# Attention scores per head in row tiles of the TensorE array, beside a mixture of experts

## The chip, the core and the metric

The kernel runs on one core of a Trainium2 chip. The time is the device time of one execution in microseconds (us). The core has five engines that run side by side: PE (TensorE, the matrix array, whose weight loads are listed as PEld), DVE (VectorE), ACT (ScalarE), POOL (GpSimd) and SP (SyncE, which here issues all DMAs).

## The reference

One layer norm feeds two branches, whose outputs are added to the input:

```python
xn = _layernorm(x, axis=-1)                    # x: 1 x 2048 x 512
# A: 32 heads of 16, causal window of 256
scores = jnp.einsum("bhqd,bhkd->bhqk", q, k) * (Dh ** -0.5)
mask = (idx[:, None] - idx[None, :] >= 0) & (idx[:, None] - idx[None, :] < W)
p = _softmax(jnp.where(mask[None, None], scores, -1e9), axis=-1)
o = jnp.einsum("bhqk,bhkd->bhqd", p, v)        # then @ wo
# B: 8 experts, F = 1376, all 8 with softmax gates
h = _silu(xf @ w1[e]) @ w2[e]
out = out + w * h
return x + _A_ref(xn, A_wqkv, A_wo) + _B_ref(xn, B_w_gate, B_w1, B_w2)
```

## The kernel before

Float32 products are made of float16 halves: each operand is split into a high and a low part, and three matmuls (high x high, high x low, low x high, `mm3`, lines 210 to 212) give one product. For the queries and keys of a head the three products are stacked along the contraction instead: 3 x 16 = 48 rows (`KR`), and two more rows (`QR` = 50) that subtract the row's maximum in the second pass.

The experts take most of the time. A loop over "doubles" (`first_products`) computes the first products with a seven-multiplication scheme (tiles zx and zy, 256 columns per matmul), and queues the second products (tile acc, 512 or 256 columns), which are drained between them. Attention is a third stream of work. It is cut into steps, and after each product `beside` lets it take as many as its share of the remaining work demands (`attend_due`). The order on every engine is worked out when the program is built: `Order` keeps a planned clock for each engine, PE matmuls advance it by a cost written beside them (`order.pe(...)`), and a step is only taken when what it needs is done by that clock. What is issued runs in that fixed order, with semaphores where a tile is handed on. Four PSUM banks (`take_bank`) are shared by the attention tiles and the experts' tanh tiles.

Attention works on one pair of heads and one half of the sequence (1024 queries) at a time: 2 x 16 passes.

- `stacks_of` loads q and k of the pair. Head a lies in rows 64a to 64a + 49. The q tile is block diagonal: its columns alternate between 64 queries of head 0 and 64 queries of head 1, and the rows of the other head are zero (`of_head` picks every second run of 64 columns). So each q load is made of pieces of 64 elements, and two ZERO loads clear the rows of the maxima.
- `att_max` finds each row's maximum. For each of 16 blocks of 64 queries one matmul (line 1947, tile sc) has 64 queries of both heads as its 128 output rows and up to 320 keys as columns; DVE adds the mask and reduces (line 1935). The maxima are transposed (tile mT, line 1954) and put into q (line 1970). This runs for the next pair beside `att_out` of the present one.
- `att_out` makes the scores again, transposed: 128 keys as output rows, and 128 or 256 queries of one head as columns (line 2072, tile st). An item of up to four 128-column pieces fills one bank and holds both heads: 11 items in the first half of the sequence, 13 in the second. ACT takes the exponential into pf (line 2028), POOL masks the newest and oldest blocks (lines 2012 and 2019), ACT makes the high part ph (line 2034), DVE or POOL the low part pl (line 2038). `LAG` items later the pv matmuls follow (line 2109, 34 columns each).
- `att_wo` projects four pairs' outputs.

The steps of `att_max` and `att_out` are interleaved by `attention`, with the constants `LEAD` and `SLACK`.

Of the kernel before, what the change touches and what calls it, by code (L numbers as in the profile page):

```python
# [10 lines left out]
F32 = mybir.dt.float32  # L11
# [32 lines left out]
LAG = 3  # L44
PB = 9
ITEMS = (11, 13)
# [7 lines left out]
LEAD = 5  # L54
SLACK = 4
# [146 lines left out]
def tile_attn_moe(ctx: ExitStack, tc: tile.TileContext, x, wqkv, wo, _bx, wg, w1, w2, out):  # L202
# [18 lines left out]
    ZERO = dram.tile([2, HALF], F16, name="ZERO")  # L221
# [305 lines left out]
    class Stream:  # L527
# [21 lines left out]
        "att": H // 2 * sum(n + QB + 2 * QB + 1 for n in ITEMS) + H // 8 * 2 * 10,  # L549
# [684 lines left out]
    for b in range(2):  # L1234

        qt = att.tile([P, 2 * HALF], F16, name=f"q{b}")
        nc.vector.memset(qt, 0.0)
        qst.append(qt)
        kt = att.tile([P, NK], F16, name=f"k{b}")
        nc.gpsimd.memset(kt, 0.0)  # L1240
        kst.append(kt)
# [14 lines left out]


    def of_head(ap, a):

        return ap.rearrange("r (b c) -> r b c", c=P)[:, :, 64 * a : 64 * a + 64]  # L1260
# [4 lines left out]
    def stacks_of(hf, p, slack):  # L1265

        s = Pair()
        s.hf, s.p = hf, p
        t0 = hf * HALF
        s.k0 = max(0, t0 - WIN)  # L1270
        s.nk = t0 + HALF - s.k0
        s.q, s.k = qst[p % 2], kst[p % 2]
        qf, kf = s.q, s.k
        s.free = [Event(order.t + DRAIN)]
        parts = []

# [12 lines left out]
        return s  # L1289

    with tc.tile_pool(name="ph0", bufs=1) as p0:
# [496 lines left out]
        def gates_out(tb, pool, tag):  # L1788
            yield [gated[tb], bank_free]
            ps, until = take_bank("gp")  # L1790
            for i in range(4):
                nc.tensor.transpose(ps[:E, i * P : (i + 1) * P], gates[:, 4 * tb + i, :], ident)

            def out():
                gs = pool().tile([P, TB], F32, tag=tag, bufs=3 if tag == "pf" else 2, name="gs")
# [39 lines left out]
        fill = p0.tile([P, 2, 20], F16, name="fill")  # L1835
        for j, (t, val) in enumerate(((ZERO, 0.0), (ONE, CO))):
            n = t.shape[0] * t.shape[1] // P
            nc.vector.memset(fill[:, j, :n], val)
            nc.sync.dma_start(t.rearrange("r t -> (r t)").rearrange("(p c) -> p c", p=P), fill[:, j, :n])
# [89 lines left out]
    def att_max(s):  # L1929
# [4 lines left out]
        def best(ps, n, j):  # L1934
            nc.vector.tensor_tensor_reduce(  # L1935
                out=ps[:, :n], in0=ps[:, :n], in1=maskf[:, MB * 64 - n :], scale=1.0, scalar=-3.0e38,
                op0=ALU.add, op1=ALU.max, accum_out=mt[:, j : j + 1],
            )

        for j in range(2 * QB):  # L1940
            jb = 2 * s.hf * QB + j
            kb = max(0, jb + 1 - MB)
            n = (jb - kb + 1) * 64
            cs = kb * 64 - s.k0
            yield [s.loaded, bank_free]
            ps, until = take_bank("sc")
            nc.tensor.matmul(  # L1947
                ps[:, :n], lhsT=s.q[:, j * P : (j + 1) * P], rhs=s.k[:, cs : cs + n], start=True, stop=True
            )
            found.append(order.task("V", 95 + n, partial(best, ps, n, j), [order.pe(n * 3 // 7)], 2500))  # L1950
            until(found[-1])
# [14 lines left out]
        def put():  # L1966
            for a in range(2):
                for r, src in enumerate((mh, ml)):
                    row = 64 * a + KR + r
                    nc.sync.dma_start(of_head(s.q[row : row + 1, :], a), src[:, 64 * a : 64 * a + 64])  # L1970
# [10 lines left out]
    def items_of(hf):  # L1981

        first, last = hf * QB, hf * QB + QB - 1
        near = {kb: [(kb, a, d) for a in range(2) for d in range(2) if first <= kb + d <= last]
                for kb in range(max(first - 1, 0), last + 1)}
        items = []
        for kb in range(max(first - 2, 0), last - 1, 2):
            items += [near.pop(n) for n in list(near) if n <= kb + 2 - (first > kb)]
            items.append([(kb + m, a, 2) for m in range(2) for a in range(2)])
        return items + list(near.values())  # L1990

    def att_out(s, quad):
# [6 lines left out]
        for n, item in enumerate(items):  # L1999
            for c, (kb, a, d) in enumerate(item):  # L2000
                place[kb, a, d] = (n, c)
                used[n] = max(used.get(n, 0), kb + d - first)
        made = []

        def selects(item, w):

            ds = [d for _, _, d in item]
            m = len(item)

            def newest():  # L2010
                pf = w["pf"][:, : m * P].rearrange("p (a c) -> p a c", a=2)[:, :, :P]
# [12 lines left out]
            return [(390, newest)] * (0 in ds) + [(610, oldest)] * (2 in ds)  # L2024

        def exp(ps, n, w):
            w["pf"] = at.tile([P, 4 * P], F32, tag="pf", bufs=3, name="pf")
# [32 lines left out]
        for n_item, item in enumerate(items):  # L2060
            n = len(item) * P
            yield [s.ready, bank_free]
            ps, until = take_bank("st")
            c = 0
            while c < len(item):
                kb, a, d = item[c]
                m = 1
                while c + m < len(item) and item[c + m][:2] == (kb, a):
# [8 lines left out]
            w = {"gone": Event()}  # L2077
            made.append(w)
            m = len(weighed)
            old = [weighed[m - 3]["low"]] if m >= 3 else []  # L2080
            t = last_exp = order.task(
                "A", 160 + n * 5 // 6, partial(exp, ps, n, w), [order.pe(n * 7 // 16), last_exp, *old], 2500
            )
            until(t)
            for cost, what in selects(item, w):
                t = order.task("G", cost, what, [t], 4000)
            old = [weighed[m - PB]["gone"]] if m >= PB else []
            if m:
                old.append(weighed[m - 1]["high"])
            w["high"] = order.task("A", 100 + n * 5 // 6, partial(high, n, w), [t, *old], 5500)  # L2090
            w["low"] = order.either({"V": 80 + n, "G": 80 + n * 41 // 20}, partial(low, n, w), [w["high"]], 7500)
            weighed.append(w)

            def whole(q):
                return max(place[k][0] for k in place if k[0] + k[2] == first + q)

            while done < QB and (n_item == len(items) - 1 or n_item >= LAG + max(whole(q) for q in range(done // GJ * GJ, done // GJ * GJ + GJ))):
                ns = sorted({place[k][0] for k in place if k[0] + k[2] == first + done})
                yield [s.v_at, *(made[i]["low"] for i in ns), *([bank_free] if done % GJ == 0 else [])]
# [5 lines left out]
                for a in range(2):  # L2105
                    ops = [(b, part) for b in kbs for part in ("hi", "lo")]
                    for n, (b, part) in enumerate(ops):
                        i, c = place[b, a, jb - b]
                        nc.tensor.matmul(  # L2109
                            pv[:, 2 * (done % GJ) + a, :], lhsT=made[i][part][:, c * P : (c + 1) * P],  # L2110
# [3 lines left out]
                for i in ns:  # L2114
                    if used[i] == done:
                        made[i]["gone"].end = ev.end
# [60 lines left out]
    def attention():  # L2177
# [8 lines left out]
        for n, (hf, p) in enumerate(todo):  # L2186
# [10 lines left out]
            speed = (2 * QB + 1 + (10 if p % 4 == 0 and n else 0)) / (steps - LEAD - SLACK)  # L2197
# [59 lines left out]
```

## Time and profile before

| | |
|---|---|
| median of 3 runs | 2098.97 us (2095.89 to 2101.11) |
| span of the profiled execution (its only time on record) | 2094.1 us |
| TensorE busy | 99% (17924 matmuls) |
| DVE, ACT, POOL busy | 80%, 67%, 53% |
| DMA | 279.29 MB, 45.7% of the 16 engines |
| granted TensorE clock | 1.00 throughout |

The span runs from the first to the last instruction. An engine's busy time is the union of its instructions; on TensorE the instructions overlap each other, and their ends are modelled. In a group's row, "x448 | 130.6, 299 | 2.0 <-DVE mt" means 448 instructions, 130.6 us busy, 299 ns for one on average, and 2.0 us in which the engine stood idle before them, most of it released by DVE's write of mt. The forms "128*128 128x320" are stationary tile (contraction rows * output rows) and output.

### The profile page before, as it was taken

What the parts mean: (1) busy time and instruction counts of PE and PEld (TensorE: products, weight loads), DVE (VectorE), ACT (ScalarE), POOL (GpSimd) and SP (SyncE); (2) the same over time, 40 slices, a digit from 0 to 9 for tenths busy, and PEclk for the clock granted to TensorE, in tenths of its full rate; (3) what the DMA queues carried; (4) which work ended last, traced back from release to release, by engine and by line L of the source; (5) the groups of instructions that cost most, each with busy time, mean ns of one, the idle gap of its engine ahead of it and who ended that gap; (6) DMA issues with size and microseconds to landing.
All of it is one profiled execution on the core that took longest, in us unless ns stands there. A gap on an engine that the chain in (4) does not pass through costs nothing.

```text
span 2094.1 us, 47341 instructions
## 1 busy us (share of the span) xinstructions
PE 2065.3 (99%) x17924; PEld 1519.3 (73%) x17924; DVE 1665.6 (80%) x3689; ACT 1408.4 (67%) x2566; POOL 1114.5 (53%) x1228
## 2 busy tenths in 40 slices
PE   7999999999999999999999999999999999999999
PEld 4656666787768876886666688667876787668865
DVE  8667777798779867987778899869978798779853
ACT  5747776567756776667758667766687667766752
POOL 5534665456635655545535655554565466555631
PEclk9999999999999999999999999999999999999999
DMA  6886444344434445344456544443444334444321
GB/s 221 259 247 202 115 142 126 80 149 132 142 83 146 117 110 150 117 118 136 114 129 188 140 135 131 131 125 99 137 147 126 101 112 134 127 117 133 87 80 51
DMA packets 287827, 279.29 MB, mean 133 GB/s; under 512 B 128328, under 2 KB 189768, under 8 KB 287600
## 3 DMA queue, kind: packets, MB, share of 16 engines
q1 hardware_dynamic: 287600, 276.28, 45.7%
q8 instruction: 140, 2.29, 0.5%
q14 instruction: 87, 0.71, 0.1%
HBM read 250.42 MB, written 25.50 MB: 132 GB/s over the span
## 4 chain that ended last, share of the span: by engine, by line
PE 79%; DVE 5%; DMA 2%; ACT 1%; SPq 1%; issue 1%; POOL 1%; DVEq 0%; POOLq 0%; ACTq 0%
PE acc L210 12%; PE acc L211 12%; PE acc L212 12%; PE zx L210 6%; PE zx L212 6%; PE zx L211 6%; PE zy L210 5%; PE zy L212 4%; PE zy L211 4%; PE st L2072 3%; PE pv L2109 3%; PE sc L1947 3%; DMA xs<-XS 1%; SPq L181 1%; PE wo L212 1%
## 5 line engine op out<-in xcount | busy, mean ns | idle before, releaser
L851 POOL TENSOR_TENSOR hl<-t,hh 128x512 f16<-128x512 f32 x232 | 281.5, 1221 | 203.0 <-ACT hh L848 189.4
L210 PE MATMUL zx<-xs,w 128*128 128x256 f16 x1376 | 374.8, 272 | 1.6 <-ACT s L989 1.1
L212 PE MATMUL zx<-xs,w 128*128 128x256 f16 x1376 | 375.0, 273 | 0.0
L211 PE MATMUL zx<-xs,w 128*128 128x256 f16 x1376 | 374.9, 272 | 0.0
L2028 ACT ACTIVATE pf<-st,esc 128x512 f32<-128x512 f32 (+1 forms) x384 | 250.6, 658 | 160.0 <-PE st L2072 146.8
L212 PE MATMUL acc<-w,hl 128*128 128x512 f16 x928 | 351.6, 379 | 0.0
L211 PE MATMUL acc<-w,hh 128*128 128x512 f16 x928 | 351.5, 379 | 0.0
L210 PE MATMUL acc<-w,hh 128*128 128x512 f16 x928 | 351.4, 379 | 0.0
L1935 DVE CUSTOM_DVE_ANT_0 sc<-sc,mask 128x320 f32<-128x320 f32 (+4 forms) x512 | 237.7, 475 | 84.6 <-PE sc L1947 82.0
L210 PEld LDWEIGHTS <-w 128*128 128x128 f16 x2408 | 235.0, 98 | 68.3 <-issue 1.8
L210 PE MATMUL zy<-xs,w 128*128 128x256 f16 x1032 | 281.1, 272 | 1.2 <-DMA xs<-XS 0.7
L211 PEld LDWEIGHTS <-w 128*128 128x128 f16 x2408 | 235.2, 98 | 63.5 <-issue 4.6
L212 PE MATMUL zy<-xs,w 128*128 128x256 f16 x1032 | 281.2, 273 | 0.0
L211 PE MATMUL zy<-xs,w 128*128 128x256 f16 x1032 | 281.2, 272 | 0.0
L212 PEld LDWEIGHTS <-w 128*128 128x128 f16 x2408 | 235.3, 98 | 27.5
L212 PEld LDWEIGHTS <-hl 128*128 128x128 f16 x1712 | 167.2, 98 | 119.5 <-issue 0.9
L2034 ACT ACTIVATE ph<-pf 128x512 f16<-128x512 f32 (+1 forms) x384 | 227.1, 601 | 34.6 <-POOL pf L2012 24.8
L2012 POOL TENSOR_SCALAR_AFFINE_SELECT pf<-pf 128x256 f32<-128x256 f32 x256 | 122.6, 480 | 220.0 <-ACT pf L2028 188.3
L2038 POOL TENSOR_TENSOR pl<-pf,ph 128x512 f16<-128x512 f32 (+1 forms) x178 | 202.2, 1141 | 57.3 <-ACT ph L2034 51.7
L210 PEld LDWEIGHTS <-hh 128*128 128x128 f16 x1712 | 167.2, 98 | 54.5 <-issue 1.3
L211 PEld LDWEIGHTS <-hh 128*128 128x128 f16 x1712 | 167.2, 98 | 53.7 <-issue 2.9
L2038 DVE TENSOR_TENSOR pl<-pf,ph 128x512 f16<-128x512 f32 (+1 forms) x206 | 155.9, 764 | 49.0 <-ACT ph L2034 48.1
(205 smaller groups left out, 4917.6 us busy)
## 6 DMA issues: line engine op xcount, KB each, us to landing
xs<-XS SPq DMA_DIRECT2D x476, 256.0 KB
r<-in_B_w_dram SPq DMA_DIRECT2D x172, 256.0 KB
r<-in_B_w_dram SPq DMA_DIRECT2D x80, 512.0 KB
q<-QS SPq DMA_DIRECT2D x192, 32.0 KB
VS<-vt SPq DMA_DIRECT2D x16, 272.0 KB
out_dram<-x SPq DMA_DIRECT2D x16, 256.0 KB
k<-KS SPq DMA_DIRECT2D x96, 40.0 KB
x<-in_A_x_dram SPq DMA_DIRECT2D x3, 1024.0 KB
```

The source lines that it names most:

```text
L210: nc.tensor.matmul(ps, lhsT=lh, rhs=rh, start=first, stop=False, **kw)
L211: nc.tensor.matmul(ps, lhsT=lh, rhs=rl, start=False, stop=False, **kw)
L212: nc.tensor.matmul(ps, lhsT=ll, rhs=rh, start=False, stop=last, **kw)
L851: nc.gpsimd.tensor_tensor(out=h["lo"], in0=h["t"], in1=h["hi"], op=ALU.subtract)
L1935: nc.vector.tensor_tensor_reduce(out=ps[:, :n], in0=ps[:, :n], in1=maskf[:, MB * 64 - n :], scale=1.0, scalar=-3.0e38, op0=ALU.add, op1=AL ...
L1947: nc.tensor.matmul(ps[:, :n], lhsT=s.q[:, j * P : (j + 1) * P], rhs=s.k[:, cs : cs + n], start=True, stop=True)
L2012: nc.gpsimd.affine_select(out=pf, in_=pf, pattern=[[0, 2], [1, P]], channel_multiplier=-1, base=0, compare_op=ALU.is_ge, fill=0.0,)
L2028: nc.scalar.activation(out=w["pf"][:, :n], in_=ps[:, :n], func=AF.Exp, bias=math.log(PSCALE), scale=esc)
L2034: nc.scalar.activation(out=w["hi"][:, :n], in_=w["pf"][:, :n], func=AF.Copy)
L2038: on(engine).tensor_tensor(out=w["lo"][:, :n], in0=w["pf"][:, :n], in1=w["hi"][:, :n], op=ALU.subtract)
L2072: nc.tensor.matmul(ps[:, c * P : (c + m) * P].rearrange("p (b c) -> p b c", c=64), lhsT=s.k[:, kc : kc + P], rhs=of_head(s.q[:, 2 * q0 * P ...
L2109: nc.tensor.matmul(pv[:, 2 * (done % GJ) + a, :], lhsT=made[i][part][:, c * P : (c + 1) * P], rhs=s.v[:, b - s.k0 // P, a * VC : (a + 1) * ...
```

## The change

The two heads of a pair are no longer put together by a block-diagonal q. The q tile holds 1024 columns, a head in its 64-row half, loaded as whole rows; ZERO, the clearing loads and the initial clearing are gone. A matmul of scores contracts over one head's 48 or 50 rows alone, so its operands start at row 0 or 64 of the array, and each head writes into its own PSUM bank. In `att_max` a step takes 128 queries: where the whole window is present, four matmuls (two heads, two halves of 64 queries that are output rows 0 to 63 and 64 to 127), else two. In `att_out` the items (6 in each half) are lists of key blocks, and each item is made for both heads, in two banks, with one exponential, one mask, one high and one low part for each head. A step waits until two banks are free (`two_free`). A second mask, `begins`, serves the first blocks. pf has 4 buffers instead of 3, ph and pl 10 instead of 9, and the constants of the order are set anew.

```diff
-LAG = 3
-PB = 9
-ITEMS = (11, 13)
+LAG = 1
+PB = 10
+PF = 4
+ITEMS = (6, 6)
...
-LEAD = 5
-SLACK = 4
+LEAD = 2
+SLACK = 2
...
+    def two_free():
+        ends = sorted(b.end for b in banks if b.end is not None)
+        return ends[1] if len(ends) > 1 else None
...
-                move(of_head(qf[part, :], a), QS[r % 2, rows, t0 : t0 + HALF].rearrange("d (b c) -> d b c", c=64))
-            move(of_head(qf[r0 + KR : r0 + QR, :], a), ZERO.rearrange("r (b c) -> r b c", c=64))
+                move(qf[part, :], QS[r % 2, rows, t0 : t0 + HALF])
...
-        for j in range(2 * QB):
-            jb = 2 * s.hf * QB + j
-            kb = max(0, jb + 1 - MB)
-            n = (jb - kb + 1) * 64
-            cs = kb * 64 - s.k0
-            yield [s.loaded, bank_free]
-            ps, until = take_bank("sc")
-            nc.tensor.matmul(
-                ps[:, :n], lhsT=s.q[:, j * P : (j + 1) * P], rhs=s.k[:, cs : cs + n], start=True, stop=True
-            )
-            found.append(order.task("V", 95 + n, partial(best, ps, n, j), [order.pe(n * 3 // 7)], 2500))
-            until(found[-1])
+        for j in range(QB):
+            jb = 2 * (s.hf * QB + j)
+            whole = jb + 1 >= MB
+            n = (MB if whole else jb + 2) * 64
+            bias = maskf if whole else beginsf[:, (MB - 1) * 64 - n :]
+            yield [s.loaded, two_free]
+            got = [take_bank("sc") for _ in range(2)]
+            for c in range(2 if whole else 1):
+                cs = max(jb + c + 1 - MB, 0) * 64 - s.k0
+                to = slice(64 * c, 64 * c + 64) if whole else slice(0, P)
+                for a in range(2):
+                    of = slice(64 * a, 64 * a + KR)
+                    nc.tensor.matmul(
+                        got[a][0][to, :n], lhsT=s.q[of, j * P + to.start : j * P + to.stop], rhs=s.k[of, cs : cs + n],
+                        start=True, stop=True,
+                    )
+            ev = order.pe(n * 3 // 7 + 40)
+            for a, (ps, until) in enumerate(got):
+                found.append(order.task("V", 95 + n, partial(best, ps, bias, a * QB + j), [ev], 2500))
+                until(found[-1])
...
+        near = [(kb, d) for kb in range(max(first - 1, 0), last + 1) for d in range(2) if first <= kb + d <= last]
+        far = [(kb, 2) for kb in range(max(first - 2, 0), last - 1)]
+        cut = 4 if hf else 3
+        near = [near[:cut], *(near[n : n + 4] for n in range(cut, len(near), 4))]
+        far = [far[:4], far[4:]]
+        return [near[0], far[0], near[1], near[2], far[1], near[3]] if hf else [*near[:2], far[0], *near[2:], far[1]]
...
-            yield [s.ready, bank_free]
-            ps, until = take_bank("st")
+            yield [s.ready, two_free]
+            got = [take_bank("st") for _ in range(2)]
...
-                nc.tensor.matmul(
-                    ps[:, c * P : (c + m) * P].rearrange("p (b c) -> p b c", c=64), lhsT=s.k[:, kc : kc + P],
-                    rhs=of_head(s.q[:, 2 * q0 * P : 2 * (q0 + m) * P], a), start=True, stop=True,
-                )
+                for a in range(2):
+                    of = slice(64 * a, 64 * a + QR)
+                    nc.tensor.matmul(
+                        got[a][0][:, c * P : (c + m) * P], lhsT=s.k[of, kc : kc + P], rhs=s.q[of, q0 * P : (q0 + m) * P],
+                        start=True, stop=True,
+                    )
...
+            ev = order.pe(n * 7 // 16 + 40)
+            made.append([])
+            for ps, until in got:
...
-            speed = (2 * QB + 1 + (10 if p % 4 == 0 and n else 0)) / (steps - LEAD - SLACK)
+            speed = (QB + 1 + (10 if p % 4 == 0 and n else 0)) / (steps - LEAD - SLACK)
```

## Rows read from the trace of the kernel before

**Rows 1.** The page: the span, TensorE's busy time (with its share and number of instructions), and the chain of work that ended last, by engine and by line.

```profile
span 2094.1 us, 47341 instructions
...
PE 2065.3 (99%) x17924; PEld 1519.3 (73%) x17924; DVE 1665.6 (80%) x3689; ACT 1408.4 (67%) x2566; POOL 1114.5 (53%) x1228
...
PE 79%; DVE 5%; DMA 2%; ACT 1%; SPq 1%; issue 1%; POOL 1%; DVEq 0%; POOLq 0%; ACTq 0%
PE acc L210 12%; PE acc L211 12%; PE acc L212 12%; PE zx L210 6%; PE zx L212 6%; PE zx L211 6%; PE zy L210 5%; PE zy L212 4%; PE zy L211 4%; PE st L2072 3%; PE pv L2109 3%; PE sc L1947 3%; DMA xs<-XS 1%; SPq L181 1%; PE wo L212 1%
```

**Rows 2.** Busy time of each engine by stretches; the columns are named in the first line (PEclk is the granted clock).

```profile
core 0: us, PE busy (x) PEld busy (x) DVE busy (x) ACT busy (x) POOL busy (x), PEclk, DMA share, GB/s
160.00:2000.00 1840.00, 1825.95 (x16395) 1371.08 (x16393) 1515.68 (x3341) 1283.73 (x2278) 1018.91 (x1120) 1.00 0.45 127
...
1100.00:1600.00 500.00, 497.20 (x4508) 375.67 (x4507) 425.75 (x930) 354.69 (x636) 281.04 (x308) 1.00 0.48 137
```

**Rows 3.** The timeline of TensorE alone around 165 us: start in us, duration in us, engine, line, operation, output and inputs, form, count.

```profile
165.40 0.27 PE L212 MATMUL zy<-xs,w 128*128 128x256 f16 x1
165.51 0.27 PE L1954 MATMUL mT<-ident,mt 128*16 128x128 f32 x1
165.62 0.27 PE L210 MATMUL zx<-xs,w 128*128 128x256 f16 x1
165.73 0.27 PE L211 MATMUL zx<-xs,w 128*128 128x256 f16 x1
...
166.82 0.27 PE L212 MATMUL zx<-xs,w 128*128 128x256 f16 x1
166.93 0.38 PE L210 MATMUL acc<-w,hh 128*128 128x512 f16 x1
```

**Rows 4.** Groups of TensorE's instructions, different shapes apart: count, busy us, mean ns of one, idle us before them.

```profile
L210 PE MATMUL zx<-xs,w 128*128 128x256 f16 x1376 | 374.8, 272 | 1.6 <-ACT s L989 1.1 <-DMA xs<-XS 0.4
...
L1947 PE MATMUL sc<-k,q 128*128 128x320 f16 x448 | 130.6, 299 | 2.0 <-DVE mt L1935 0.8 <-ACT pf L2028 0.5 <-DMA q<-ZERO 0.5
...
L2109 PE MATMUL pv<-v,pl 128*128 128x34 f16 x1440 | 102.1, 177 | 1.5 <-DVE pl L2038 1.5
...
L2072 PE MATMUL st<-q,k 128*128 128x256 f16 x448 | 82.2, 272 | 1.0 <-DMA q<-ml 1.0
L2072 PE MATMUL st<-q,k 128*128 128x128 f16 x544 | 55.1, 219 | 0.0
...
L1947 PE MATMUL sc<-k,q 128*128 128x256 f16 x16 | 4.4, 272 | 0.0
L1947 PE MATMUL sc<-k,q 128*128 128x192 f16 x16 | 3.9, 246 | 0.3 <-DVE mt L1935 0.3
L1947 PE MATMUL sc<-k,q 128*128 128x128 f16 x16 | 3.5, 219 | 0.0
L1947 PE MATMUL sc<-k,q 128*128 128x64 f16 x16 | 3.1, 192 | 3.5 <-DMA q<-ZERO 1.4 <-ACT ph L2034 1.3 <-PE zx L212 0.4
```

**Rows 5.** The timeline around 1003.5 us, TensorE's rows: sc and st matmuls between those of the experts.

```profile
1003.37 0.30 PE L1947 MATMUL sc<-k,q 128*128 128x320 f16 x1
...
1003.50 0.39 PE L2072 MATMUL st<-q,k 128*128 128x128 f16 x4
...
1003.73 0.43 PE L1947 MATMUL sc<-k,q 128*128 128x320 f16 x2
...
1004.00 0.38 PE L210 MATMUL acc<-w,hh 128*128 128x512 f16 x1
```

**Rows 6.** The timeline of TensorE around 1974.5 us: pv matmuls (24 of them up to the mT), the mT transpose and what follows.

```profile
1974.34 0.18 PE L2109 MATMUL pv<-v,ph 128*128 128x34 f16 x1
1974.37 0.18 PE L2109 MATMUL pv<-v,pl 128*128 128x34 f16 x1
...
1974.92 0.18 PE L2109 MATMUL pv<-v,pl 128*128 128x34 f16 x1
1974.95 0.27 PE L1954 MATMUL mT<-ident,mt 128*16 128x128 f32 x1
1975.06 0.27 PE L210 MATMUL acc<-w_0C,hh 128*128 128x256 f16 x1
```

**Rows 7.** TensorE's waits: who was waited for, us in total, how often, the longest.

```profile
PE sc L1947 <- DMA q<-ZERO: 1.9, 4, 0.6
```

**Rows 8.** Groups of the engines that read and mask the scores, columns as in rows 4.

```profile
L1935 DVE CUSTOM_DVE_ANT_0 sc<-sc,mask 128x320 f32<-128x320 f32 x448 | 217.6, 497 | 68.8 <-PE sc L1947 66.6
...
L1935 DVE CUSTOM_DVE_ANT_0 sc<-sc,mask 128x64 f32<-128x64 f32 x16 | 3.6, 228 | 9.0 <-PE sc L1947 9.0
...
L2028 ACT ACTIVATE pf<-st,esc 128x512 f32<-128x512 f32 x336 | 228.5, 685 | 131.2 <-PE st L2072 118.2 <-POOL pl L2038 6.6 <-DVE pl L2038 4.1
L2028 ACT ACTIVATE pf<-st,esc 128x256 f32<-128x256 f32 x48 | 22.6, 471 | 28.8 <-PE st L2072 28.5
...
L2012 POOL TENSOR_SCALAR_AFFINE_SELECT pf<-pf 128x256 f32<-128x256 f32 x256 | 122.6, 480 | 220.0 <-ACT pf L2028 188.3 <-PE sc L1947 20.3 <-DVE t L835 9.8
L2019 POOL TENSOR_SCALAR_AFFINE_SELECT pf<-pf 128x512 f32<-128x512 f32 x112 | 78.2, 698 | 116.9 <-ACT pf L2028 93.5 <-PE sc L1947 10.9 <-DVE t L835 10.8
```

**Rows 9.** DMA issues by line: count and size of each.

```profile
q<-QS SPq DMA_DIRECT2D x192, 32.0 KB
...
q<-ZERO SPq DMA_DIRECT2D x64, 4.0 KB
```

More of the change, by code (lines that the diff above doesn't have):

```diff
@@ L548, in tile_attn_moe @@
     left = {
-        "att": H // 2 * sum(n + QB + 2 * QB + 1 for n in ITEMS) + H // 8 * 2 * 10,
+        "att": H // 2 * sum(n + QB + QB + 1 for n in ITEMS) + H // 8 * 2 * 10,
         "groups": sum((14 + q) * p for q, p in zip(quotas, pace)),
@@ L1255, in tile_attn_moe @@
     maskf = mask.rearrange("p a b -> p (a b)")
-    def of_head(ap, a):
-        return ap.rearrange("r (b c) -> r b c", c=P)[:, :, 64 * a : 64 * a + 64]
+    begins = att.tile([P, MB - 1, 64], BF16, name="begins")
+    nc.gpsimd.memset(begins, 0.0)
+    nc.gpsimd.memset(begins[:64, MB - 2, :], NEG)
+    for a in range(2):
+        half = begins[64 * a : 64 * a + 64, MB - 3 + a, :]
+        nc.gpsimd.affine_select(
+            out=half, in_=half, pattern=[[-1, 64]], channel_multiplier=1, base=0, compare_op=ALU.is_ge, fill=NEG,
+        )
+    beginsf = begins.rearrange("p a b -> p (a b)")
     class Pair:
@@ L1834, in tile_attn_moe @@
         nc.vector.memset(eps, 1e-5)
[L1835 to L1839, printed above, removed]
+        fill = p0.tile([P, 2 * NK // P], F16, name="fill")
+        nc.vector.memset(fill, CO)
+        nc.sync.dma_start(ONE.rearrange("r t -> (r t)").rearrange("(p c) -> p c", p=P), fill)
         for kt in kst:
@@ L1999, in att_out @@
         for n, item in enumerate(items):
-            for c, (kb, a, d) in enumerate(item):
-                place[kb, a, d] = (n, c)
+            for c, (kb, d) in enumerate(item):
+                place[kb, d] = (n, c)
                 used[n] = max(used.get(n, 0), kb + d - first)
@@ L2005, in selects @@
         def selects(item, w):
-            ds = [d for _, _, d in item]
             m = len(item)
+            ds = [d for _, d in item]
             def newest():
-                pf = w["pf"][:, : m * P].rearrange("p (a c) -> p a c", a=2)[:, :, :P]
+                pf = w["pf"].rearrange("p (a b c) -> p a b c", a=2, b=2)[:, :, ds.index(0), :]
                 nc.gpsimd.affine_select(
@@ L2061, in att_out @@
             n = len(item) * P
-            yield [s.ready, bank_free]
-            ps, until = take_bank("st")
+            yield [s.ready, two_free]
+            got = [take_bank("st") for _ in range(2)]
             c = 0
             while c < len(item):
-                kb, a, d = item[c]
+                kb, d = item[c]
                 m = 1
-                while c + m < len(item) and item[c + m][:2] == (kb, a):
+                while c + m < len(item) and item[c + m][0] == kb:
                     m += 1
@@ L2084, in att_out @@
[L2084 to L2092, printed above, removed]
+                for a in range(2):
+                    of = slice(64 * a, 64 * a + QR)
+                    nc.tensor.matmul(
+                        got[a][0][:, c * P : (c + m) * P], lhsT=s.k[of, kc : kc + P], rhs=s.q[of, q0 * P : (q0 + m) * P],
+                        start=True, stop=True,
+                    )
@@ new lines, in att_out @@
+                c += m
+            ev = order.pe(n * 7 // 16 + 40)
+            made.append([])
+            for ps, until in got:
+                w = {"gone": Event()}
+                made[-1].append(w)
+                m = len(weighed)
+                old = [weighed[m - PF]["low"]] if m >= PF else []
+                t = last_exp = order.task("A", 160 + n * 5 // 6, partial(exp, ps, n, w), [ev, last_exp, *old], 2500)
+                until(t)
+                for cost, what in selects(item, w):
+                    t = order.task("G", cost, what, [t], 4000)
+                old = [weighed[m - PB]["gone"]] if m >= PB else []
+                if m:
+                    old.append(weighed[m - 1]["high"])
+                w["high"] = order.task("A", 100 + n * 5 // 6, partial(high, n, w), [t, *old], 5500)
+                w["low"] = order.either({"V": 80 + n, "G": 80 + n * 41 // 20}, partial(low, n, w), [w["high"]], 7500)
+                weighed.append(w)
@@ L2094, in whole @@
             def whole(q):
-                return max(place[k][0] for k in place if k[0] + k[2] == first + q)
+                return max(place[k][0] for k in place if sum(k) == first + q)
             while done < QB and (n_item == len(items) - 1 or n_item >= LAG + max(whole(q) for q in range(done // GJ * GJ, done // GJ * GJ + GJ))):
-                ns = sorted({place[k][0] for k in place if k[0] + k[2] == first + done})
-                yield [s.v_at, *(made[i]["low"] for i in ns), *([bank_free] if done % GJ == 0 else [])]
+                ns = sorted({place[k][0] for k in place if sum(k) == first + done})
@@ L2100, in att_out @@
+                yield [s.v_at, *(w["low"] for i in ns for w in made[i]), *([bank_free] if done % GJ == 0 else [])]
                 if done % GJ == 0:
@@ L2115, in att_out @@
                     if used[i] == done:
-                        made[i]["gone"].end = ev.end
+                        for w in made[i]:
+                            w["gone"].end = ev.end
                 if done % GJ == GJ - 1:
```

42 lines of the change are left out of this document (13 added, 29 removed).

## The prediction

> **What bounds the kernel now.** I read the page first, its busy times and the chain of waits [rows 1]. TensorE is busy for 2065.3 of 2094.1 us, and 79% of the chain is its matmuls; no other engine is above 80%. So the question is whether TensorE is merely occupied or really full. The table by stretch [rows 2] shows that from 160 to 2000 us it is busy for 1825.95 of 1840 us, at a granted clock of 1.00 (the 2.4 GHz level). A matmul's duration in the trace overlaps the next one's, so I take prices from starts. In [rows 3] twelve 256-column matmuls start between 165.62 and 166.93: 1.31 us / 12 = 109 ns each. Their row says 272 ns [rows 4]: 109 ns of streaming and 163 to 164 ns under way while the next already runs. The same subtraction gives 135 ns for 320 columns (299 - 164) and 55 ns for 128 columns (219 - 164), and the starts agree: in [rows 5] two sc matmuls take 1004.00 - 1003.73 = 0.27 us, and four 128-column st matmuls 0.23 us. The pv matmuls of 34 columns start 25 ns apart: 24 from 1974.34 to 1974.95 [rows 6]. No bubbles are left: score matmuls follow projections and the other way round at once. TensorE is the bound, and a column less is time less as long as the order keeps feeding it.
>
> **What the change removes and adds, on TensorE.** The score matmuls of now, by the counts of [rows 4] and steps of duration less 164 ns:
> - sc (the pass for the maxima): 448 x 135 ns, and 16 each of 256, 192, 128 and 64 columns (108, 82, 55 and 28 ns; 192 lies between the others): 64.8 us.
> - st (the pass for the probabilities): 448 x 108 + 544 x 55 ns = 78.3 us.
>
> Together 143.1 us, 6.8% of the span; the chain's 3% + 3% says the same [rows 1].
>
> After the change each head has 64 rows of the array for itself, so the two heads' matmuls can stream side by side. In the maxima pass the two halves of 128 queries take two column halves as well, so four matmuls of 320 columns can fill the array at once. By the new loops, for each pair of heads:
> - sc: in the first half of the sequence 6 of 8 blocks have the whole window, in the second all 8; over 16 pairs 224 groups of four, 135 ns each. The first two blocks are groups of two, 128 and 256 columns: 16 x (55 + 108) ns. Sum 32.8 us.
> - st: the runs with one key block in the new lists, for one head: 4 of 256 and 13 of 128 columns in the first half, 4 and 16 in the second; 16 x (8 x 108 + 29 x 55) ns = 39.3 us.
>
> Perfectly side by side that is 72.2 us, a gain of 70.9 us.
>
> **Stagger.** Matmuls still start one after the other. The nearest price is the pv row's 25 ns between starts [rows 6]. A group of four then ends 75 ns after a lone one would, a group of two (the second head trailing the first) 25 ns: 224 x 75 + (32 + 192) x 25 ns = 22.4 us. Below, it could be nothing. The Trainium skill ("TensorE: Matmul & The Clock Gate", Part 3, measured speedup) gives about 4 ns per further tile; by that figure, as an estimate, the term would be 3.6 us and the forecast 19 us lower. No row here shows two tiles at once, so I keep 25 ns in the sum.
>
> **Change of the array's shape.** Each of the 256 + 192 = 448 groups stands between full-array matmuls, so the array is re-divided and restored, up to 896 edges. No row shows 64-row tiles. The nearest is mT, whose stationary tile is 128x16: it starts 25 ns after the last pv, and its successor 0.11 us after it [rows 6]; in [rows 3] it also fits without a gap. So the lower end is 0. The upper end is that nothing may be under way at an edge: 164 ns x 896 = 147 us. I take 0, by the mT row, and keep the other end: it is the largest unknown here. The break-even is close, as the rivals show.
>
> **Waits.** A group now asks for two free PSUM banks, and the second bank is read only after the first (497 ns for a 320-column reduction, 685 ns for a 512-column exp [rows 8]). TensorE's present idle time before sc, st and pv is about 8 us in these rows [rows 4], of which 1.9 us is for the q<-ZERO transfers that go away [rows 7]. I add 5 us. Bounds: -2 us (only the ZERO waits vanish) and +30 us (its 14 us of idle time in 160 to 2000 us trebled).
>
> **The other engines**, all at nothing, because TensorE covers them:
> - DVE: the reductions stay 512, two per block and pair. Only the first blocks grow, by 128 columns per pair in the first half; at (497 - 228) / 256 = 1.05 ns a column [rows 8] that is 2.1 us. DVE is busy for 1515.68 of 1840 us [rows 2]; with 44 us less span it goes from 82 to 84%.
> - ACT: 384 exps as before (32 of 384, 32 of 256, 320 of 512 columns): some 2 us more. POOL: the mask of the near blocks stays 256 times; the far one goes from 112 of 512 to 96 of 512 and 32 of 256 columns: 96 x 698 + 32 x 480 = 82.4 against 78.2 us [rows 8]. Both have a quarter of their time free. If that cover were gone, the three would cost 2 + 2 + 4 us.
> - SP: 64 q<-ZERO issues vanish, and the 192 q<-QS loads become whole rows, in place of pieces of 64 elements [rows 9]. This frees the queue and the DMA engines. Nothing on TensorE waited for it beyond the 1.9 us, so it earns no more.
>
> The pv matmuls, their 2880 x 25 ns, are untouched. The smaller lag and lead constants move work in the order, but add none to TensorE.
>
> **Sum.** -70.9 + 22.4 + 0 + 5 = -43.5 us on a span of 2094.1. The record has no time of the profiled execution but its span; the median of the runs, 2098.97, lies 4.9 us above, and I carry that distance over: 2098.97 - 43.5 = 2055.5 us.
>
> **Rivals.**
> - Drain at the edges: each change of the array's division waits for what is under way. For it: 163 ns of every matmul lie behind the next one's start [rows 3, 4], so there is something to wait for; against it: mT costs nothing, though it changes columns and not rows. It beats the gain from 43.5 us / 448 = 97 ns per group (49 ns an edge). At 164 ns an edge: 2055 + 147 = 2202 us; at 75 ns an edge: 2055 + 67 = 2122 us. The Trainium skill ("TensorEngine Tiling (Array Packing)", Key Properties) says that changing the tiling mode, though not changing only the tile, drains TensorE. The Trainium skill ("TensorE: Matmul & The Clock Gate", Part 2, step DRAIN) puts the way through the array at about 128 cycles, which at 2.4 GHz would be, as an estimate, 53 ns an edge: about no change. No run here shows it yet.
> - The tiles don't run at once: the matmuls stream in turn. Then sc costs 224 x 4 x 135 + 32 x (55 + 108) ns = 126.2 us instead of 64.8, and st stays: +61.4 + 5, about 2165 us. For it: no row shows two matmuls streaming together.
> - The gain is given back as waits: TensorE runs out of work, because two banks must come free together or because DVE, at 85% in 1100 to 1600 us [rows 2], is late. At +30 us instead of +5: 2080 us; to reach 2099 the idle time would have to grow to four times. Against it: 14 us of idle time in 1840.
>
> **Chances.** Forecast 0.55 (own range 2032 to 2078, which holds a stagger of nothing and up to 50 ns of drain a group), drain at the edges beyond break-even 0.23, tiles in turn 0.06, given back as waits 0.16 (most of it still faster). About no change means within 0.3%, some 6 us, which is what a measurement of this kernel can tell; the drain near break-even and the worst of the waits share 0.08. Faster 0.65, same 0.08, slower 0.27. Below 2030 us both stagger and waits would have to be nothing (0.04). The range goes up to 2132 us: it takes in drains up to 85 ns an edge and leaves out the harder ones and the tiles in turn (0.15).
>
> **What would show it.** Right: the two heads' score matmuls start some 25 ns apart and overlap; a whole sc group takes 0.2 us to the next full-array start, a st item 0.25 us (sc now 0.27 for the same work, st 0.43); TensorE's idle time stays under 20 us; sc and st fall from 6% to 4 or 5% of the chain. Wrong: a gap at the first and last matmul of each group, with weight loads that start only then; starts 135 ns apart inside a group; or new waits on `two_free` banks, seen as idle time before sc and st released by DVE or ACT.

## The result and the profile after

The changed kernel takes 2108.03 us in the median of 4 runs (2107.63 to 2109.26) against 2097.43 for the kernel before on the same chip: 1.0053 times as long, with a 95% interval from 1.0039 to 1.0068. I had forecast 2055.5 us, and 2030 to 2132 as the range. So the time lies in the range, on the wrong side: 0.5% slower in place of 2% faster.

The page of the changed kernel, with the lines that answer to [rows 1]:

```profile
span 2105.9 us, 48812 instructions
...
PE 2082.5 (99%) x18564; PEld 1429.0 (68%) x18564; DVE 1632.1 (78%) x3657; ACT 1409.4 (67%) x2566; POOL 1133.4 (54%) x1275
...
PE 92%; DVE 5%; DMA 1%; ACT 1%; issue 1%; POOL 0%; SPq 0%; DVEq 0%; ACTq 0%
```

TensorE is still the bound, and more so: 92% of the chain in place of 79%. The table by stretch, as in [rows 2], says the same:

```profile
160.00:2000.00 1840.00, 1832.27 (x16901) 1275.82 (x16900) 1475.92 (x3294) 1276.75 (x2265) 1030.99 (x1155) 1.00 0.43 127
```

TensorE's idle time in that stretch fell from 14 to 8 us, at the same clock, and the span still grew. Then its own work must have grown. Its groups by shape, answering to [rows 4]:

```profile
L1954 PE MATMUL sc<-k,q 48*64 48x320 f16 x896 | 73.2, 319 | 0.3 <-DVE mt L1937 0.2
L2085 PE MATMUL st<-q,k 50*128 50x128 f16 x928 | 70.5, 220 | 0.1
L2085 PE MATMUL st<-q,k 50*128 50x256 f16 x256 | 35.2, 270 | 0.6 <-DMA q<-ml 0.5
```

These rows mislead if read alone. The counts are those of the forecast (224 x 4 = 896, 29 x 2 x 16 = 928, 8 x 2 x 16 = 256), the idle time before them is nothing, and sc's busy time even fell from 130.6 to 73.2 us. What they cannot show is time in which an earlier matmul still counts as busy while no column streams. For that the timeline is needed, with the weight loads (PEld) beside the matmuls:

```profile
1003.76 0.27 PE L211 MATMUL zx<-xs,w 128*128 128x256 f16 x1
1003.76 0.10 PEld L212 LDWEIGHTS <-w 128*128 128x128 f16 x1
1003.87 0.27 PE L212 MATMUL zx<-xs,w 128*128 128x256 f16 x1
1003.87 0.10 PEld L213 LDWEIGHTS <-w 128*128 128x128 f16 x1
1003.97 0.27 PE L213 MATMUL zx<-xs,w 128*128 128x256 f16 x1
1004.17 0.17 PEld L2085 LDWEIGHTS <-k 50*128 50x128 f16 x6 [0.21 <-issue]
1004.18 0.40 PE L2085 MATMUL st<-q,k 50*128 50x128 f16 x6
1004.50 0.11 PEld L1954 LDWEIGHTS <-q 48*64 48x64 f16 x4 [0.16 <-issue]
1004.50 0.33 PE L1954 MATMUL sc<-k,q 48*64 48x320 f16 x4
1004.76 0.10 PEld L211 LDWEIGHTS <-w 128*128 128x128 f16 x1
1004.77 0.28 PE L211 MATMUL zy<-xs,w 128*128 128x256 f16 x1
1004.78 0.10 PEld L212 LDWEIGHTS <-w 128*128 128x128 f16 x1
1004.89 0.27 PE L212 MATMUL zy<-xs,w 128*128 128x256 f16 x1
```

The last zx starts at 1003.97 and has streamed its 256 columns at 1004.08. The st group starts at 1004.18, 0.10 us later. Among the zx, a weight load starts with the matmul before it; here it starts with its own group, after 0.21 us of "issue", that is, idle time for which the profile shows no cause. The same happens from st to sc (half tiles to quarter tiles: 0.32 us for 0.22 us of columns) and from sc back to the full array (0.27 us for 0.135 us). Two groups of the same division, however, follow each other without a pause:

```profile
1000.71 0.38 PE L213 MATMUL acc<-w,hl 128*128 128x512 f16 x1
...
1001.02 0.40 PE L2085 MATMUL st<-q,k 50*128 50x128 f16 x8
...
1001.25 0.27 PE L1954 MATMUL sc<-k,q 48*128 48x256 f16 x2
...
1001.46 0.39 PE L211 MATMUL acc<-w,hh 128*128 128x512 f16 x1
```

The st group (half tiles) takes 0.23 us for 512 columns of each head, and the sc of half tiles behind it starts at once; before the one and behind the other 0.10 us are lost. So the price is paid where the division of the array into tiles changes: from the full array to row tiles and back, and from half to quarter tiles, which both have 64 rows and differ in their output columns. The trace does not tell whether the array has to empty first or whether it is the weight load (0.10 us in these rows) that is no longer hidden.

To put a number on it I add up, over all matmuls in the trace, the time from each start to the next. A full-array matmul is charged its columns at 2.4 GHz and 2.5 ns more, at least 25 ns, which gives the steps of the rows before (109 ns for 256 columns in [rows 3], 25 ns in [rows 6]); a float32 transposition is charged 109 ns, as mT in [rows 3]. What is left before a row-tiled group counts as its entry up to 100 ns, and as a wait beyond; a group runs from its first start to the next full-array start.

| us | score matmuls, with edges | waits of TensorE | first to last matmul |
|---|---|---|---|
| before | 65.3 sc + 79.3 st = 144.6 | 31.7 | 2083.6 |
| after | 127.2 in groups + 39.2 entry + 4.6 slower first matmuls after them = 171.0 | 17.4 | 2095.4 |

26.4 - 14.3 = 12.1 us, against 11.8 us measured from first to last matmul (the 4.6 us are 418 groups at the median of 11 ns). The two have to agree nearly, because these classes leave no time out; what the sum tells is where the time went. Some 3 us of the 127.2 are waits inside a few groups: their time above the median of groups of the same make. Medians from the same starts: entry 96 ns for half tiles (93 for quarter tiles); an st item of 512 columns takes 231 ns if another half-tiled group follows and 327 ns if the full array does, so 96 ns for the exit; for sc in quarter tiles 136 ns (two groups in a row take 398, one 262) and 262, so 126 ns; and the first full-array matmul after a group takes 11 ns longer. Together 203 ns a group for st and 230 ns for sc.

### The profile page after: what moved, and what is told of

It is laid out like the page before. It is cut to its first block, busy times and chain, and to the rows that moved or that the text cites. A ratio compares the mean times of both kernels' runs of the same rounds, so it can differ in the third digit from the quotient of the medians.

```text
span 2105.9 us, 48812 instructions
## 1 busy us (share of the span) xinstructions
PE 2082.5 (99%) x18564; PEld 1429.0 (68%) x18564; DVE 1632.1 (78%) x3657; ACT 1409.4 (67%) x2566; POOL 1133.4 (54%) x1275
## 4 chain that ended last, share of the span: by engine, by line
PE 92%; DVE 5%; DMA 1%; ACT 1%; issue 1%; POOL 0%; SPq 0%; DVEq 0%; ACTq 0%
PE acc L211 14%; PE acc L212 13%; PE acc L213 13%; PE zx L211 7%; PE zx L213 7%; PE zx L212 7%; PE zy L211 5%; PE zy L213 5%; PE zy L212 5%; PE qk L1654 4%; PE pv L2123 3%; PE sc L1954 3%; PE st L2085 3%; PE vg L1717 2%; DVE x L731 1%
## 5 line engine op out<-in xcount | busy, mean ns | idle before, releaser
L855 POOL TENSOR_TENSOR hl<-t,hh 128x512 f16<-128x512 f32 x232 | 274.1, 1190 | 237.3 <-ACT hh L852 225.9
L2039 ACT ACTIVATE pf<-st,esc 128x512 f32<-128x512 f32 (+2 forms) x384 | 244.1, 657 | 151.8 <-PE st L2085 149.7
L2049 POOL TENSOR_TENSOR pl<-pf,ph 128x512 f16<-128x512 f32 (+2 forms) x211 | 237.3, 1134 | 60.8 <-ACT ph L2045 57.0
L1937 DVE CUSTOM_DVE_ANT_0 sc<-sc,mask 128x320 f32<-128x320 f32 x448 | 211.4, 511 | 58.7 <-PE sc L1954 56.7
L2045 ACT ACTIVATE ph<-pf 128x512 f16<-128x512 f32 (+2 forms) x384 | 224.3, 602 | 10.1 <-POOL pf L2030 4.9
L2023 POOL TENSOR_SCALAR_AFFINE_SELECT pf<-pf 128x256 f32<-128x256 f32 x256 | 116.7, 461 | 168.5 <-ACT pf L2039 165.5
L731 DVE SCALAR_TENSOR_TENSOR x<-acc,gsc,x 128x256 f32<-128x256 f32 x280 | 175.3, 635 | 23.8 <-PE acc L213 22.9
```

Source lines behind the costliest of these rows:

```text
L731: nc.vector.scalar_tensor_tensor(out=dst, in0=src, scalar=backs[g][:, 4 * tb + row : 4 * tb + row + 1], in1=dst, op0=ALU.mult, op1=ALU.add,)
L855: nc.gpsimd.tensor_tensor(out=h["lo"], in0=h["t"], in1=h["hi"], op=ALU.subtract)
L1937: nc.vector.tensor_tensor_reduce(out=ps[:, :n], in0=ps[:, :n], in1=bias, scale=1.0, scalar=-3.0e38, op0=ALU.add, op1=ALU.max, accum_out=mt ...
L2023: nc.gpsimd.affine_select(out=pf, in_=pf, pattern=[[0, 2], [1, P]], channel_multiplier=-1, base=0, compare_op=ALU.is_ge, fill=0.0,)
L2039: nc.scalar.activation(out=w["pf"][:, :n], in_=ps[:, :n], func=AF.Exp, bias=math.log(PSCALE), scale=esc)
L2045: nc.scalar.activation(out=w["hi"][:, :n], in_=w["pf"][:, :n], func=AF.Copy)
```

## The experiments

Theory 1 is the price at the edges. Theory 2 puts the loss on the new structure: one-head tiles, two banks, the new order. Theory 3 is that the tiles take turns. Each run was compared with the kernel before on the same chip.

### One-head tiles in the full array

```diff
-                    of = slice(64 * a, 64 * a + QR)
+                    of = slice(0, P)
...
-        for j in range(QB):
+        for j in range(2 * QB):
...
-PB = 10
-PF = 4
+PB = 9
+PF = 3
```

> Score tiles hold one head in att_out, two banks at a time, with the changed kernel's items, lag, lead and slack; but q is block diagonal again, st contracts over all 128 rows and sc is that of before: no row tiles at all (pf has 3 buffers and ph/pl 9, as q needs the room). Theory 1 (each change between full-array and row-tiled matmuls costs TensorE some 96 ns going in and 120 ns coming out): no such change is left and TensorE's score work is that of before, so the time is that of before within 6 us, 2091 to 2103. Theory 2 (the one-head items, the two banks and the new order cost the time): it stays where the changed kernel is, 2105 or more. Theory 3 (the row tiles do not overlap): 2091 to 2103 as well.

2100.89 us, 1.0016 [1.0007, 1.0024] of before. With no row tiles most of the loss is gone. Here q is block diagonal again, and `att_max` (second part of the diff) is the kernel before's. The sum over starts gives 145.1 us for the score matmuls, as before, and 35.0 us of waits. The structure costs some 3 us by itself and not 11: theory 2 explains little.

### Row tiles for st alone

```diff
-                    of = slice(0, P)
+                    of = slice(64 * a, 64 * a + QR)
...
-            ev = order.pe(n * 7 // 8)
+            ev = order.pe(n * 7 // 16 + 40)
```

> As a_one_head_full_array, but the st matmuls contract over one head's 50 rows, in row tiles; sc stays in the full array. Theory 1: an item of 512 columns takes 327 ns to the next start plus 96 ns before it and 11 after, against 436: nearly even. By the changed kernel's own group times 16 x (1800 + 1968 + 12 x 107) ns = 80.8 us against 78.3 us: 2 to 3 us above a_one_head_full_array. Theory 3: st stays at 78 us and the edges come on top: 192 x 0.2 = 40 us above it. Theory 2: no difference.

The diff is against the run before this, whose other edits stay. 2104.16 us (1.0036 [1.0022, 1.0050]), 3.3 us above that run. The score matmuls take 143.8 us (some items met without an edge, 176 groups for 192 items), the waits 40.9. So half the columns go and as much comes back at the edges: for st the change is near a draw, and its tiles do run at once, against theory 3.

### Quarter tiles for sc alone

```diff
+            for c in range(2):
+                to = slice(64 * c, 64 * c + 64)
+                for a in range(2):
+                    of = slice(64 * a, 64 * a + KR)
+                    nc.tensor.matmul(
+                        got[a][0][to, :n], lhsT=s.q[of, (2 * j + c) * P + 64 * a : (2 * j + c) * P + 64 * a + 64],
+                        rhs=s.k[of, cs : cs + n], start=True, stop=True,
+                    )
```

> As a_one_head_full_array, but the maxima pass is the changed kernel's: 128 queries a step, four matmuls (two heads, two halves of 64 queries) in quarter tiles, each head into its own bank, for the first blocks too; st stays in the full array. Theory 1: a group takes 262 ns to the next start plus 93 before and 11 after it, 366 against 270 ns: 224 x 96 ns = 21.5 us, and the 32 short groups some 5 us: 26 us above a_one_head_full_array, so the maxima pass holds the whole loss. Theory 3: four times 135 ns plus edges, 224 x 0.48 = 107 us above. Theory 2: no difference.

The diff shows the lines put in, against the first of these runs. 2149.86 us (1.0251 [1.0236, 1.0267]), 49 us above that run, where I had expected 26. The sum over starts splits the miss: the score matmuls take 178.6 us, 33.5 more than in the first run, and the waits 49.6, 14.6 more. Of the 33.5 us some 7 are waits inside groups, which leaves the 26 that I had expected: before, this work cost 270 ns for 128 queries of a pair, now 366. The waits were not in my sum. One row of them has grown from 2.1 us in the first run:

```profile
PE acc L211 <- DVE x L732: 13.0, 15, 4.2
```

The experts' second products waited for DVE. And in five stretches, 23.8 us together, the granted clock stood at its lower level (1.2 GHz). Each of them comes behind or amid waits of TensorE (ahead of the one below it had waited 1.49 us for ACT, up to 1167.79 us):

```profile
1168.90:1172.30 3.40, 3.40 (x15) 2.00 (x14) 3.40 (x10) 3.37 (x7) 2.22 (x3) 0.50 0.87 278
```

(The clock is the third figure from the end.) The full-array matmuls in the five stretches take 9.8 us longer than the sum charges, and it counts that among the waits. The mean granted clock of this run is 0.994, that of the first run 1.00. Why the order of this run brings the waits about stays open.

### The edges doubled, and a control

```diff
+                if c == len(item) // 2 or (c < len(item) // 2 < c + m):
+                    nc.tensor.matmul(
+                        got[0][0][:, c * P : c * P + 64], lhsT=s.k[0:P, kc : kc + P], rhs=s.q[0:P, q0 * P : q0 * P + 64],
+                        start=True, stop=True,
+                    )
```

> The changed kernel with one matmul more in each st item, of 64 columns over all 128 rows, put between the item's row-tiled matmuls (its output is overwritten by the next of them; the tiles of q and k are cleared once at the start). In 176 items it lies inside, so the array goes back to full and to row tiles once more; in 16 it lies ahead. Theory 1 (the edges cost): 176 x (96 + 109 + 11 + 29) + 16 x 29 ns = 44 us more than the changed kernel, 2152. Rival (the edges are free, what costs is the order and its waits): 192 x 29 ns = 6 us, 2114.

> The same as e_edges_doubled, but the matmul of 64 columns contracts over 50 rows from row 0, so it stays in row tiles and adds no edge. Theory 1: 192 x some 30 ns = 6 us more than the changed kernel, 2114. Rival (any further matmul there costs what e_edges_doubled costs): the same time as e_edges_doubled.

The diff is that of the doubled edges; the control has `0:QR` in place of `0:P`. 2147.47 us with the full-array matmul and 2114.00 with the row-tiled one (2 runs each). Against the changed kernel's 2108.03 us the control adds 6 us, as expected; the same columns over the full array add 39 us (44 expected). The timeline with the edges doubled (L2088 is the added matmul):

```profile
1009.87 0.38 PE L213 MATMUL acc<-w,hl 128*128 128x512 f16 x1
1010.18 0.23 PE L2094 MATMUL st<-q,k 50*128 50x128 f16 x2
1010.34 0.20 PE L2088 MATMUL st<-q,k 128*128 128x64 f16 x1
1010.48 0.34 PE L2094 MATMUL st<-q,k 50*128 50x256 f16 x4
1010.75 0.28 PE L211 MATMUL zx<-xs,w 128*128 128x256 f16 x1
```

and of the control:

```profile
1020.87 0.23 PE L2094 MATMUL st<-q,k 50*128 50x128 f16 x2
1020.93 0.19 PE L2088 MATMUL st<-q,k 50*128 50x64 f16 x1
1020.93 0.35 PE L2094 MATMUL st<-q,k 50*128 50x256 f16 x4
```

Within the row tiles the first pair of 128 columns takes 0.06 us, and the added matmul makes the item 26 ns longer (353 in place of 327 ns). With the full array between, the pair takes 0.16 us and the 64 columns 0.14: 0.10 us for each change, in an item that is otherwise the same. In the sum over starts, the 176 further entries come to 17.6 us and the groups' time with the exits to 17.5 us more, the added columns themselves to 5.6 us, and the waits stay (16.5 for 17.4 us). The price of an edge is shown.

### The plan's price for an edge

The order is planned with 40 ns for a group's edges. Does it matter that the chip takes 200?

```diff
-            ev = order.pe(n * 3 // 7 + 40)
+            ev = order.pe(n * 3 // 7 + 220)
...
-            ev = order.pe(n * 7 // 16 + 40)
+            ev = order.pe(n * 7 // 16 + 220)
```

> The changed kernel with one thing altered: the order is worked out with 220 ns more for each group of row-tiled matmuls in place of 40, about what the trace shows. The matmuls are the same, their order can move. Theory 1 (TensorE itself is longer, whatever the plan says): same time as the changed kernel within 5 us, 2103 to 2113. Rival (the plan's clock runs ahead of the chip, and the order that it makes is bad): the time falls to that of before or below, 2098 or less.

2132.36 us (1.0170 [1.0156, 1.0183]): neither. The true price in the plan made the kernel 24 us slower than the false one. The waits are 32.3 us, up from 17.4, and another 10 us stand inside the groups. That suggested a reason why the changed kernel waits less than the one before, and a test on the kernel before:

```diff
-        self.t += cost
+        self.t += cost * 24 // 25
```

> The kernel before, with the order worked out for a TensorE that is 4% faster than it is (each of its costs x 24/25); nothing else. It tests why the changed kernel's waits fell from 31.7 to 17.4 us although its matmuls grew: its plan prices a group 180 ns too low, some 80 us or 4% over the span, so what a step needs is done earlier than TensorE gets there. If that is the reason: waits fall by about 14 us here too, 2083. If the fall came from the changed kernel's items, buffers or loads: no change, 2097.

2097.57 us (1.0005 [0.9995, 1.0014]), waits 33.7 us: no change, so this test gives that reason no support. Three more prices for the changed kernel:

> The changed kernel with a planned price of 0 in place of 40 ns for a group's edges. If too low a price keeps TensorE's waits low: waits 17 us or less, 2105 to 2108. If the waits scatter with any change of the order, whatever its sign: anywhere between 2105 and 2132.

> The same with 100 ns. If the waits follow the price: between the changed kernel (40 ns, 2108) and h_planned_edges (220 ns, 2132), about 2116. If they scatter: anywhere between 2105 and 2132.

> The same with 160 ns. If the waits follow the price: about 2124, above h_price_100. If they scatter: anywhere between 2105 and 2132.

2113.93, 2117.81 and 2116.15 us (2 runs each) for 0, 100 and 160 ns, beside 2108.03 for 40 and 2132.36 for 220. These runs are of three chips; each against the kernel before on its own chip, they are 1.0070, 1.0053, 1.0088, 1.0080 and 1.0170 for 0, 40, 100, 160 and 220 ns. There is no clear order in them from 0 to 160 (the intervals of 0 and 40 ns overlap): an altered plan moves this kernel by up to some 10 us, and 220 ns by 24. At 0 ns the waits are 20.5 us, where the reason above asked for 17 or less.

### Fewer edges: both passes in one division

```diff
+        if len(tiled) == 2 and order.met([four_free, *tiled[0].needs[:1], *tiled[1].needs[:1]]):
+            assert go(tiled[0])
+            joined[0] = True
+            assert go(tiled[1])
...
+            n = min(MB + 1, jb + 2) * 64
+            for a in range(2):
+                of = slice(64 * a, 64 * a + KR)
+                nc.tensor.matmul(
+                    got[a][0][:, :n], lhsT=s.q[of, j * P : (j + 1) * P], rhs=s.k[of, cs : cs + n], start=True, stop=True
+                )
```

> The changed kernel with fewer edges. The maxima pass uses half tiles as the other pass does (two matmuls of 128 queries and up to 384 keys), so both passes share one division of the array, and where a step of each can be taken and four banks are free they are issued together; the order then has 308 groups in place of 432. Theory 1: 308 x 216 ns of edges + 40.3 us for sc + 41.7 us for st = 148.5 us of TensorE in place of 171, so 22 us less than the changed kernel if its waits stay: 2086, within 8, below the kernel before. Rival (the gain is eaten: DVE reads 64 columns more in 448 reductions, some 30 us, and four banks at once hold up the experts): waits grow by as much, 2108 or more.

2098.86 us (1.0010 [1.0001, 1.0019]): 9 us below the changed kernel, level with the one before. TensorE did what was expected: 308 groups, 149.9 us of score matmuls (148.5 expected). A joined group:

```profile
1020.95 0.38 PE L215 MATMUL acc<-w,hl 128*128 128x512 f16 x1
1021.26 0.40 PE L2107 MATMUL st<-q,k 50*128 50x128 f16 x6
1021.49 0.33 PE L1977 MATMUL sc<-k,q 48*128 48x384 f16 x2
1021.75 0.28 PE L213 MATMUL zx<-xs,w 128*128 128x256 f16 x1
```

st takes 0.23 us and is followed at once by sc. But the waits rose from 17.4 to 29.8 us, so 12 of the 21 us saved were given back.

### A version that beats both: two st items to a group

sc, which lost in quarter tiles, stays in the full array; two st items are issued as one step. The diff is against the run with row tiles for st alone, and the two `while` lines are cut short.

```diff
-            yield [s.ready, two_free]
+            if n_item % 2 == 0:
+                yield [s.ready, four_free]
...
-            while done < QB and (n_item
+            while n_item % 2 and done < QB and (n_item
...
-ITEMS = (6, 6)
+ITEMS = (3, 3)
...
-            ev = order.pe(n * 7 // 16 + 40)
+            ev = order.pe(n * 7 // 16 + 110)
```

> b_st_rows_only with two consecutive st items issued as one step that waits for four free banks: 96 groups of row-tiled matmuls, each between full-array ones, in place of 176, and the plan prices their edges (220 ns a group). sc stays in the full array. Theory 1: the edges fall by 80 x 216 ns = 17 us at least against b_st_rows_only, so about 2087, within 10 for the waits: below both kernels if the waits stay near b_st_rows_only's 41 us. Rival (four banks at once hold up the experts' tanh, and four exponentials in a row make DVE and pv late): waits grow by 17 us or more, 2104 or above.

2086.76 us, 0.9939 [0.9924, 0.9954] of before, as expected: 0.6% faster. One of its groups:

```profile
1006.55 0.38 PE L213 MATMUL acc<-w,hl 128*128 128x512 f16 x1
1006.86 0.62 PE L2091 MATMUL st<-q,k 50*128 50x128 f16 x14
1007.41 0.39 PE L211 MATMUL acc<-w,hh 128*128 128x512 f16 x1
```

1024 columns of each head take 0.55 us with the exit, after an entry of 0.10 us; the full array needs 4 x 0.22 us. The 96 groups cost 64.7 us with their edges, against 79.3 for st before. The waits (38.5 us) give back half of it.

## Why the prediction was wrong

- **The bound: right.** TensorE was full, and the difference in time lies in its work and its waits.
- **The gain from columns (-70.9 us): right in mechanism and size.** Without edges the row-tiled work would be 224 x 136 + 16 x (66 + 120) ns for sc and 41.9 us for st, by the group times that end in the same division: 75.4 us for the 72.2 forecast.
- **Stagger (22.4 us): mis-sized.** The pv row's 25 ns was the wrong neighbour. The four matmuls of a quarter-tile group start 3 to 4 ns apart (in the one at 528.57 us: 0, 4, 7 and 10 ns after the first), and the term comes to 75.4 - 72.2 = 3.2 us (the first step inside a group is also some 11 ns longer than the later ones: in the st group at 1004.18 us 67 ns for 128 columns). The Trainium skill's 4 ns, which I had quoted from "TensorE: Matmul & The Clock Gate" (Part 3, measured speedup), agrees with the trace.
- **Change of the array's shape ("I take 0, by the mT row"): the step that failed.** It cost 171.0 - 75.4 = 95.6 us (some 3 of them waits inside groups), more than the whole gain. The mT row was true and did not bear on the question: mT uses 16 output columns of the array but all its rows, and it costs nothing extra after the change either:

```profile
161.58 0.27 PE L213 MATMUL zy<-xs,w 128*128 128x256 f16 x1
161.69 0.27 PE L1964 MATMUL mT<-ident,mt 128*16 128x128 f32 x1
161.80 0.27 PE L211 MATMUL zx<-xs,w 128*128 128x256 f16 x1
```

Every edge that cost time has a row tile on at least one side. Few output columns alone were no sign of one, and I had no other row. The forecast's 448 groups became 418, because some met another. I had put the break-even at 97 ns a group; a group's edges cost 203 to 230 ns. The rival "drain at the edges" was the right one as to the cost. I had cited for it from "TensorEngine Tiling (Array Packing)" in the Trainium skill (Key Properties) that a change of the tiling mode drains TensorE and a change of tile alone does not; the trace agrees as to the time (0.10 us against no gap above), and no run here shows that it is a drain. The estimate that I had worked out from "TensorE: Matmul & The Clock Gate" in the Trainium skill (Part 2, step DRAIN), 53 ns, is about half of what an edge costs here (93 to 126 ns).

- **Waits (+5 us): wrong in sign.** They fell by 14.3 us between the groups, with some 3 us of new ones inside groups. The doubt about two free banks did not come true in the changed kernel: the rows of sc and st have less than 2 us of idle time before them. Why the waits fell is open: nothing shows that it was the plan's price (the kernel before did not gain from a plan 4% too fast), and the one-head items alone did not do it (35.0 us in the full array). The runs that have whole-row q loads and the changed kernel's sc and st have 16 to 22 us, and 32 at a planned price of 220; the joined groups, with whole-row loads too, have 29.8; those with block-diagonal q have 32 to 50. The loads and the buffers were not tried alone.
- **The other engines at nothing: right.** DVE is at 78%, with 5% of the chain before and after; the q<-ZERO waits are gone.
- **A slip in a rival.** For waits that undo the gain the prediction said four times the 14 us of idle time; by its own terms it is 14 + 5 + 43.5 us, four and a half times.

The chance of 0.23 on that rival was too low: the one row I had for an edge was of another kind, and the other end of the bounds, 147 us, was more than three times the 43.5 us that would undo the gain.

## What to carry to other kernels

Splitting the array into row tiles pays by the stretch spent in them: each way in and out costs TensorE about 0.1 us here, so a group must save more than 0.2 us of columns. With half tiles 512 columns of each of two heads were near a draw and 1024 won; quarter tiles with 320 columns, in place of two full-array matmuls of 320, lost; group the tiled work, keep one division, and leave short pieces in the full array. When TensorE's busy time is near 100%, look for such losses in the starts of the timeline, not in busy or idle times.

## What the runs showed that I had not expected

- An edge is no idle time in the rows: the earlier matmul still counts as busy, and what shows is the later start and a weight load that starts with its matmul, after "issue", in place of one matmul ahead.
- A change between half and quarter tiles costs as much as one to the full array: an st item of 512 columns takes 325 ns before a quarter-tile sc (7 cases), 327 before the full array and 231 before a half-tiled sc. Both kinds of tile have 64 rows, so it is not the number of rows alone that counts.
- The first full-array matmul after a row-tiled group takes 120 ns to the next start in place of 109.
- Behind a wait inside a group the clock fell. With the planned price of 220 ns, the second of two sc matmuls at 752.59 us waited 1.93 us until ACT wrote pf from a bank; in the stretch behind it the granted clock was at its lower level (1.2 GHz):

```profile
750.00:753.00 3.00, 1.07 (x8) 0.36 (x6) 1.00 (x2) 1.55 (x4) 1.13 (x2) 1.00 0.48 179
753.00:756.50 3.50, 3.50 (x17) 1.53 (x16) 3.37 (x8) 3.41 (x8) 3.08 (x4) 0.51 0.00 0
```

TensorE was busy for 1.07 of 3 us in the first of the two stretches (the third column; the clock is the third from the end), and in the second its 256-column matmuls start 0.21 us apart in place of 0.11. The wait is part of the 10 us that stand inside the groups of that run; what the matmuls behind it lose is counted among its waits.
